# Later loads behind w_k's split, an early Exp table and a later bias split at the start of an attention, MoE and mixer kernel

## The chip, the core and the metric

The kernel runs on one core of a Trainium2 chip. The metric is the device time of one execution in microseconds: 876.57 us is the median of three runs of the kernel before (875.78 to 877.5). One more execution was profiled; it took 876.73 us, of which the trace covers a span of 875.0 us.

## The reference

Three blocks follow each other: causal attention with a cumulative bias, a gated feed-forward block (called MoE in the names) and a token and channel mixer. All numbers are fp32.

```python
def _attn_ref(q, k, v, s):            # 4 batches, 8 heads, 576 tokens, head size 64
    scores = scale * np.matmul(q, k.transpose(0, 1, 3, 2))
    cum = np.cumsum(np.maximum(s, 0.0), axis=-1)
    bias = -(cum[:, :, :, None] - cum[:, :, None, :])
    scores = np.where(causal, -1000000000.0, scores + np.minimum(bias, 0.0))
    attn = softmax(scores)            # written out in the reference
    return np.matmul(attn, v)

def _moe_ref(x, mu_k, mu_r, w_k, w_v, w_r):    # model 512, hidden 1024
    xk = mu_k * x + (1.0 - mu_k) * x_prev      # x_prev: the token before
    xr = mu_r * x + (1.0 - mu_r) * x_prev
    k = np.maximum(xk @ w_k, 0.0)
    return 1.0 / (1.0 + np.exp(-(xr @ w_r))) * (k * k @ w_v)

def _moe2_ref(x, w_tok1, w_tok2, w_ch1, w_ch2):
    u = x + (np.maximum(xt @ w_tok1, 0.0) @ w_tok2).transpose(0, 2, 1)
    return u + np.maximum(u @ w_ch1, 0.0) @ w_ch2
```

## The kernel before, in words

Most products are made of three: both operands are split into a high and a low fp32r word, and high by high, high by low and low by high are summed in PSUM (`products`, line 103). A weight arrives as a raw block and is split in `weight_split` (line 600): ScalarE copies the scaled high halves (line 604 or 607, both through `copy`, line 75) and rewrites the low halves (line 609), VectorE joins them in two passes (lines 610 and 611), ScalarE writes the high words (line 612) and GpSimd the low words (line 616; for w_v VectorE, line 614). Where `ps` is given, the scaled high halves go into one of two PSUM banks (`ps_w`), else back in place into SBUF.

Batch 0's attention is done apart from the rest, head by head, and in two parts. `early` (line 330) takes the first 256 query rows of a head (items j of 0 and 1): scores with the bias as two more rows of the contraction, maximum and mask on VectorE (line 276), Exp on ScalarE (line 287), row sums and normalisation on GpSimd (lines 288 and 290), transposes on TensorE, a copy T on ScalarE and the product with V (line 355). `late` (line 377) takes the other 320 rows, with four bias rows that `split_bias` (line 189) makes and stores in DRAM (`ext_d`). `split_bias` runs in three chunks through a tile `e` of one buffer: GpSimd writes its ones, VectorE its words, and ScalarE's queue issues the store (line 200).

Between them `mix` (line 503) makes HX, the mixed input of w_k's products for two heads at a time. `up` (line 514) multiplies it by w_k; its products are called h. `gate` and `down` (products r and vd) use w_r and w_v. `keep_busy` (line 159) gives TensorE products that nobody reads, here called fillers: 13 at the start, and four behind each early item.

Each engine and each DMA queue takes its instructions in the order in which they stand. That order is made by a scheduler from the data dependences, buffers and the priorities that `at(place)` sets; a lower place comes earlier. Loads are issued on SyncE's queue (SP). The lines of the change: `late_load` (line 364) and `late_values` (line 369) bring q, k, bias and v for a late head, `weight_load` (line 586) a raw weight block. A load can be made to wait by writing a word into its target with an instruction that waits for something, as `behind` (line 156) does. Late head h uses the tile X of slot h % 4; slots 2 and 3 are used before by the early heads 4 to 7. w_k and w_r come in 8 and 4 blocks of 512 KB through five buffers, w_v in 16 blocks through the pool `xt`.

Of the kernel before, what the change touches and what calls it, by code (L numbers as in the profile page):

```python
# [24 lines left out]
def attention_moe_mixer(  # L25
# [118 lines left out]
    xt = {}  # L144
# [13 lines left out]

    def keep_busy(n, x, w):
        idle = ps_t.tile([128, 512], F32, tag="t", name="idle")  # L160
        for _ in range(n):
            nc.tensor.matmul(idle[:, 0:w], x[:, 0:128], x[:, 0:w], start=True, stop=True)
# [26 lines left out]
    def split_bias(cp, cum):  # L189
        n = 3  # L190
        for c in range(n):
            a, z = S * c // n, S * (c + 1) // n
            e = cp.tile([G, 4, 2, z - a], F32R, name="e")
            for r, t in ((1, 1), (3, 1), (0, 0), (2, 0)):
                nc.gpsimd.memset(f32(e[:, r, t, :]), 1.0)
            copy("D", e[:, 0, 1, :], cum[:, a:z])
            nc.vector.tensor_tensor(out=e[:, 2, 1, :], in0=cum[:, a:z], in1=f32(e[:, 0, 1, :]), op=ALU.subtract)
            for x in (0, 2):
                copy("D", e[:, x + 1, 0, :], f32(e[:, x, 1, :]), -1.0)
            nc.scalar.dma_start(out=ext_d[:, :, :, a:z], in_=f32(e))  # L200
# [129 lines left out]
    def early(h, j, V0, cp):  # L330
# [7 lines left out]
        softmax(j, P, mx, 0)  # L338
        if j == 0:
# [24 lines left out]
    def late_load(h):  # L364
        x = late_x[h] = x_tile(h % 4)
        nc.sync.dma_start(out=x[0:D], in_=qk[h])
        nc.sync.dma_start(out=x[D:D + 4], in_=ext_d[h])

    def late_values(p):
        t = v_tile(p % 2)  # L370
        n = S // 128
        nc.sync.dma_start(out=t[:, 0:n], in_=v[0, 0:128 * n, 2 * p * D:(2 * p + 2) * D].rearrange("(t p) d -> p t d", p=128))
# [213 lines left out]
    def weight_load(key, sw, n, pool, tag, q=nc.sync, after=None):  # L586
        r, k, f = sw.shape
        t = pool.tile([128, n, 2], I32, tag=tag, name="raw")[:, 0:k * f].rearrange("p (k f) t -> p k f t", f=f)
        if after is not None:
            behind(after, f32(t[0:1, 0, 0:1, 0]))  # L590
        for r0 in range(0, 128, r):
# [115 lines left out]
    nc.vector.memset(maskc, 0.0)  # L707
    ps_s2, ps_w = open_pool(name="ps_w", bufs=2, space=PSUM, reuse_waits="tile")
    keep_busy(13, maskc, 512)
# [40 lines left out]
    with at(2):  # L750
        split_bias(cp, cum)
    with at(N0 - 5):
        for h in range(4):
            late_load(h)
        for p in range(2):
            late_values(p)
    x = 1.0
    for y, a in enumerate(first):
# [4 lines left out]
        with at(x + 0.6):  # L763
            weight_split((nm, f), W[:, 0, :, f:f + 128], W[:, 1, :, f:f + 128], ps=ps_w)
        x += 1.2
    cp_s.close()
# [12 lines left out]
    for f in range(0, DM, 128):  # L779
        for k in range(0, KF, 2):  # L780
            with at(x):
                weight_load((k, f), rows(w_v, k, k + 2)[:, :, f:f + 128], S // 2, xt_p, "xt")
# [236 lines left out]
```

## Time and profile before

| | |
|---|---|
| median of 3 runs | 876.57 us (875.78 to 877.5) |
| profiled execution | 876.73 us, span 875.0 us |
| TensorE busy | 842.1 us, 96% of the span |
| weight loads of TensorE | 790.2 us, 90% |
| VectorE, ScalarE, GpSimd busy | 480.6, 451.4, 336.9 us |
| share of the chain that ended last | TensorE 37%, ScalarE and VectorE 2% each |

TensorE is the engine that is nearly always busy. A busy share does not say how much work is done: the granted clock has to be read beside it, and fillers count as busy. The page's slices of the span (about 22 us each) show TensorE's gaps in the first three slices and between 140 and 300 us. The DMA line has its highest shares in the first slices too.

### The profile page before, as it was taken

To read this page: it belongs to the slowest core of one execution; us is meant where nothing else is said; L and a number is where in the kernel's file an instruction comes from. 1 tells how busy PE (TensorE), PEld (TensorE's weight loads), DVE (VectorE), ACT (ScalarE), POOL (GpSimd) and SP (SyncE) were. 2 spreads that over 40 slices of the span, in tenths; PEclk is the share of its full clock that TensorE was granted. 3 is DMA by queue.
4 is the path that set the end of the run, shared out by engine and by line. 5 is a ranking of instruction groups with operands and counts; after the bars stand their busy time and mean duration, and the time that the engine had idled before them with its cause. 6 is when DMAs were issued, how large, how long until landed. Compare 5 with 4: busy or idle time off the path is not lost. (4 is left out here: it accounts for less than half of the span.)

```text
span 875.0 us, 17439 instructions
## 1 busy us (share of the span) xinstructions
PE 842.1 (96%) x6125; PEld 790.2 (90%) x6125; DVE 480.6 (55%) x1351; ACT 451.4 (52%) x1256; POOL 336.9 (39%) x600
## 2 busy tenths in 40 slices
PE   7989998988899999999999999999999999999998
PEld 5746767988689999999999989899999999999998
DVE  4877775656769556985469766961331222222221
ACT  3888766856786755868477864840310211211210
POOL 3654766855774644645255854730000000000000
PEclk7989999999999999999999999999999999999999
DMA  7963597887975244431234746562022112112100
GB/s 184 241 169 92 164 248 214 220 229 209 249 196 130 71 106 112 109 91 43 62 104 135 225 150 198 177 197 90 10 85 60 41 34 67 43 37 69 42 25 25
DMA packets 88023, 108.34 MB, mean 124 GB/s; under 512 B 11152, under 2 KB 71568, under 8 KB 87936
## 3 DMA queue, kind: packets, MB, share of 16 engines
q1 hardware_dynamic: 81408, 91.56, 37.6%
q0 software_dynamic: 4576, 15.08, 5.4%
q8 instruction: 48, 0.79, 0.4%
q10 hardware_dynamic: 1952, 0.60, 0.4%
q14 instruction: 39, 0.32, 0.1%
HBM read 77.74 MB, written 28.90 MB: 122 GB/s over the span
## 5 line engine op out<-in xcount | busy, mean ns | idle before, releaser
L858 ACT ACTIVATE HID<-c 128x256 fp32r<-128x256 f32 (+1 forms) x96 | 39.3, 409 | 220.3 <-PE c L108 220.2
L108 PE MATMUL vd<-KK,WV 128*128 128x256 f32 (+1 forms) x768 | 120.2, 300 | 0.9 <-ACT e L536 0.8
L108 PEld LDWEIGHTS vd<-KK,WV 128*128 128x128 f32 x768 | 106.4, 188 | 4.7 <-issue 1.6
L108 PE MATMUL h<-XK,WK 128*128 128x320 f32 (+1 forms) x672 | 105.8, 301 | 3.3 <-ACT k L521 1.9
L290 POOL TENSOR_SCALAR P<-P,sum 128x128 f32<-128x128 f32 (+4 forms) x148 | 91.9, 624 | 42.2 <-DVE sum L289 32.4
L108 PE MATMUL c<-HID,WV 128*128 128x256 f32 (+1 forms) x768 | 104.9, 291 | 0.0
L108 PE MATMUL c<-U,WK 128*128 128x256 f32 (+1 forms) x768 | 103.2, 291 | 1.4 <-DVE HID L859 1.4
L108 PEld LDWEIGHTS c<-HID,WV 128*128 128x128 f32 x768 | 100.6, 188 | 0.0
L108 PEld LDWEIGHTS c<-U,WK 128*128 128x128 f32 x768 | 98.6, 188 | 1.7 <-DVE HID L859 1.6
L108 PEld LDWEIGHTS h<-XK,WK 128*128 128x128 f32 x672 | 93.2, 188 | 5.5 <-ACT k L521 3.3
L287 ACT ACTIVATE P<-P,mx 128x128 f32<-128x128 f32 (+4 forms) x148 | 86.6, 587 | 21.1 <-DVE mx L276 19.3
L859 DVE SCALAR_TENSOR_TENSOR HID<-c,HID 128x256 fp32r<-128x256 f32 (+1 forms) x96 | 43.8, 456 | 81.1 <-ACT HID L858 81.0
L276 DVE CUSTOM_DVE_ANT_0 P<-s,maskc 128x128 f32<-128x128 f32 (+4 forms) x148 | 69.4, 480 | 33.5 <-PE t L430 19.1
L923 DVE TENSOR_TENSOR ut<-c,ut 128x256 f32<-128x256 f32 (+1 forms) x32 | 14.6, 458 | 119.2 <-PE c L108 109.1
L108 PE MATMUL r<-XR,WR 128*128 128x320 f32 (+1 forms) x384 | 61.9, 301 | 0.0
L288 POOL TENSOR_SCALAR sum<-sum 128x1 f32<-128x1 f32 (+1 forms) x148 | 31.8, 215 | 76.2 <-ACT P L287 68.7
L524 POOL TENSOR_TENSOR KK<-k,KK 128x256 fp32r<-128x256 f32 (+1 forms) x64 | 53.7, 844 | 16.1 <-ACT k L523 15.3
L108 PE MATMUL c<-HID,WR 128*128 128x256 f32 (+1 forms) x384 | 54.8, 291 | 0.0
L108 PEld LDWEIGHTS r<-XR,WR 128*128 128x128 f32 x384 | 53.4, 188 | 1.1 <-ACT k L523 0.2
L108 PE MATMUL c<-U,C1A 128*128 128x256 f32 (+1 forms) x384 | 52.8, 296 | 0.1
L108 PEld LDWEIGHTS c<-U,C1A 128*128 128x128 f32 x384 | 51.5, 190 | 0.3 <-ACT U L908 0.3
L108 PEld LDWEIGHTS c<-HID,WR 128*128 128x128 f32 x384 | 51.4, 188 | 0.0
(130 smaller groups left out, 1653.8 us busy)
## 6 DMA issues: line engine op xcount, KB each, us to landing
X<-hl_d SPq DMA_DIRECT2D x72, 288.0 KB
hl_d<-PB SPq DMA_DIRECT2D x48, 288.0 KB
raw<-in_moe_w_ch_dram POOLq DMA_DIRECT2D x48, 256.0 KB, 3.4
PB<-in_qk_dram SPq DMA_DIRECT2D x48, 144.0 KB
yt<-y_d SPq DMA_DIRECT2D x16, 288.0 KB
u_d<-yt SPq DMA_DIRECT2D x16, 288.0 KB
raw<-in_moe_w_k_dram SPq DMA_DIRECT2D x8, 512.0 KB
raw<-in_moe_w_v_dram SPq DMA_DIRECT2D x16, 256.0 KB
```

The lines of the kernel that those rows point to most:

```text
L108: nc.tensor.matmul(ps, a, b, start=first and i == 0, stop=last and i == n - 1)
L276: nc.vector.tensor_tensor_reduce(out=P[0:m, c0:c1], in0=ps[0:m, 0:c1 - c0], in1=mask[0:m], scale=-scale, scalar=3.0e38 if x == 0 else mx[0 ...
L287: nc.scalar.activation(out=P[0:m, 0:w], in_=P[0:m, 0:w], func=AF.Exp, bias=mx[0:m, x:x + 1], scale=-1.0, accum_out=sm[0:m, 0:1])
L288: nc.gpsimd.tensor_scalar(out=sm[0:m, 0:1], in0=sm[0:m, 0:1], scalar1=1e-9, scalar2=1.0, op0=ALU.add, op1=ALU.mult)
L290: nc.gpsimd.tensor_scalar(out=P[0:m, 0:w], in0=P[0:m, 0:w], scalar1=sm[0:m, 1:2], scalar2=1.0, op0=ALU.mult, op1=ALU.mult)
L524: nc.gpsimd.tensor_tensor(out=kk[:, 1, m, 0:n], in0=t[:, 0:n], in1=f32(kk[:, 0, m, 0:n]), op=ALU.subtract)
L858: nc.scalar.activation(out=hi, in_=ps, func=AF.Relu)
L859: nc.vector.scalar_tensor_tensor(out=lo, in0=ps, scalar=0.0, in1=f32(hi), op0=ALU.max, op1=ALU.subtract)
L923: nc.vector.tensor_tensor(out=t, in0=ps, in1=t, op=ALU.add)
```

## The change

Six edits are made together, all at the start of the program.

- `after_block(y, cell)` copies one low word of w_k's block y into a cell on GpSimd. The late loads of heads 0 and 1 and of the values of pairs 0 and 1 get such a word from block 2 in their targets; the w_v loads placed before 20 get one from block 6.
- The late loads' code stands behind that of the weight blocks.
- `split_bias` is called inside `early`, behind the softmax of head 0's first item, and its first chunk waits for a word of that item's tile P.
- An Exp on eight columns of `omu` comes first on ScalarE, so the table is loaded there; `omu` is cleared for it.
- 15 fillers instead of 13 at the start.
- w_r's scaled high halves stay in SBUF instead of a bank.

```diff
+    def after_block(y, cell):
+        nc.gpsimd.tensor_copy(cell, f32(wk[0:1, 1, KD - 1, 128 * y:128 * y + 1]))
...
-    def split_bias(cp, cum):
+    def split_bias(cp, cum, behind):
...
             e = cp.tile([G, 4, 2, z - a], F32R, name="e")
+            if c == 0:
+                nc.gpsimd.tensor_copy(f32(e[0:1, 0, 1, 0:1]), behind)
...
         softmax(j, P, mx, 0)
+        if h == 0 and j == 0:
+            with at(2):
+                split_bias(cp, cum, P[0:1, 0:1])
...
         x = late_x[h] = x_tile(h % 4)
+        if h < 2:
+            after_block(2, x[0:1, 0, 0:1])
...
         n = S // 128
+        if p < 2:
+            after_block(2, t[0:1, 0, 0:1])
+            after_block(2, t[0:1, n, 0:1])
...
+        if gate is not None:
+            after_block(gate, f32(t[0:1, 0, 0:1, 0]))
...
     nc.vector.memset(maskc, 0.0)
+    nc.vector.memset(omu, 0.0)
     ps_s2, ps_w = open_pool(name="ps_w", bufs=2, space=PSUM, reuse_waits="tile")
-    keep_busy(13, maskc, 512)
+    nc.scalar.activation(out=omu, in_=omu, func=AF.Exp)
+    keep_busy(15, maskc, 512)
...
-    with at(2):
-        split_bias(cp, cum)
-    with at(N0 - 5):
-        for h in range(4):
-            late_load(h)
-        for p in range(2):
-            late_values(p)
     x = 1.0
...
-            weight_split((nm, f), W[:, 0, :, f:f + 128], W[:, 1, :, f:f + 128], ps=ps_w)
+            weight_split((nm, f), W[:, 0, :, f:f + 128], W[:, 1, :, f:f + 128], ps=ps_w if nm == "k" else None)
         x += 1.2
+    with at(N0 - 5):
+        for h in range(4):
+            late_load(h)
+        for p in range(2):
+            late_values(p)
...
-                weight_load((k, f), rows(w_v, k, k + 2)[:, :, f:f + 128], S // 2, xt_p, "xt")
+                weight_load((k, f), rows(w_v, k, k + 2)[:, :, f:f + 128], S // 2, xt_p, "xt", gate=6 if x < 20 else None)
```

The scheduler makes a new order of the first third of the program from this. Three places of it follow; line numbers are those of each kernel's own file, the changed one's being 3 to 15 higher.

VectorE at the start, before: the bias row sums (st), the first two chunks of the bias split (e), then the maximum of the first scores (P_161).

```order
L180 SCALAR_TENSOR_TENSOR st<-st 32x320
L77 CAST e<-st 32x192
L77 COPY V_145<-e_129 32x1
L167 TENSOR_SCALAR omu<-mu 128x8
L197 TENSOR_TENSOR e<-st,e 32x192
L79 TENSOR_SCALAR e<-e 32x192 x2
L77 CAST e<-st 32x192
L197 TENSOR_TENSOR e<-st,e 32x192
L79 TENSOR_SCALAR e<-e 32x192 x2
L276 ISA P_161,mx<-s,maskc 128x128
```

The same place of the changed kernel, from omu to the first chunk of the bias split.

```order
L170 TENSOR_SCALAR omu<-mu 128x8
L281 ISA P_165,mx<-s,maskc 128x128
L281 ISA mx 128x1
L281 ISA P_213,mx<-s,maskc 128x256
L281 ISA mx 128x1
L281 ISA P_247,mx<-s,maskc 128x128
L281 ISA mx 128x1
L294 RECIPROCAL sum<-sum 128x1
L281 ISA P_264,mx<-s,maskc 128x256
L281 ISA mx 128x1
L294 RECIPROCAL sum<-sum 128x1
L77 CAST e<-st 32x192
```

The four first maxima have moved ahead of the bias split, whose first chunk now stands behind two row sums' reciprocals.

SyncE's queue from w_k's block 1 on, before; X_544, X_547 and X_550 are the tiles of late heads 0, 1 and 2, ext_d the stored bias rows.

```order
L592 DMA raw<-in_moe_w_k_dram 128x4x256 x4
L366 DMA X_544<-in_qk_dram 64x1152
L592 DMA raw<-in_moe_w_k_dram 128x4x256
L367 DMA X_544<-ext_d 4x1152
L366 DMA X_547<-in_qk_dram 64x1152
L367 DMA X_547<-ext_d 4x1152
L372 DMA VV_556<-in_v_dram 128x4x128
L366 DMA X_550<-in_qk_dram 64x1152
L367 DMA X_550<-ext_d 4x1152
```

In the changed kernel X_651 and X_655 are late heads 0 and 1, X_659 and X_662 late heads 2 and 3, and VS holds the values of a later batch.

```order
L607 DMA raw<-in_moe_w_k_dram 128x4x256 x4
L248 DMA VS<-in_v_dram 128x4x128
L607 DMA raw<-in_moe_w_k_dram 128x4x256
L250 DMA VS<-in_v_dram 64x128 x2
L376 DMA X_659<-in_qk_dram 64x1152
L607 DMA raw<-in_moe_w_k_dram 128x4x256 x2
L376 DMA X_662<-in_qk_dram 64x1152
L376 DMA X_651<-in_qk_dram 64x1152
L377 DMA X_651<-ext_d 4x1152
L376 DMA X_655<-in_qk_dram 64x1152
L607 DMA raw<-in_moe_w_r_dram 128x4x256
```

All eight w_k blocks are now issued ahead of the first late bias row; late heads 2 and 3 stand ahead of heads 0 and 1.

TensorE around the first products h, before; P_945 is a tile of a late head, PT its transposes.

```order
L387 MATMUL s<-X_550 128x384
L387 MATMUL s<-X_550 128x512
L387 MATMUL s<-X_550 64x288
L396 MATMUL t<-ident,P_945 128x128 x3
L416 MATMUL pv<-PT_821,VV_556 64x320 x3
L416 MATMUL pv<-PT_821,VV_556 64x192
L416 MATMUL pv<-PT_821,VV_556 64x64
L387 MATMUL s<-X_550 64x288
L108 MATMUL h<-HX,WK 128x256 x20
```

In the changed kernel the first products h stand among the last early heads; P_503 and P_520 are tiles of early head 6, X_655 is late head 1.

```order
L400 MATMUL s<-X_655 128x384
L165 MATMUL idle<-P_481 128x128 x4
L108 MATMUL h<-HX,WK 128x256 x7
L400 MATMUL s<-X_655 128x512
L108 MATMUL h<-HX,WK 128x256 x5
L400 MATMUL s<-X_655 64x288
L352 MATMUL t<-ident,P_503 128x128
L352 MATMUL t<-ident,P_520 128x128 x2
L363 MATMUL pv<-T,V_149 64x256
L363 MATMUL pv<-T,V_149 64x128
L165 MATMUL idle<-P_503 128x128 x4
L108 MATMUL h<-HX,WK 128x256 x6
```

18 products h have moved from behind the first late PV to places ahead of the last early head's PV.

## Rows read from the trace of the kernel before

**Rows 1.** Stretches: length, busy us (count) of PE, PEld, DVE, ACT, POOL, clock, DMA.

```profile
0.00:8.00 8.00, 6.19 (x19) 2.61 (x19) 3.96 (x13) 0.00 (x0) 3.08 (x19) 1.00 0.44 82
8.00:14.40 6.40, 2.93 (x8) 2.28 (x9) 2.71 (x14) 3.07 (x10) 1.71 (x7) 0.57 1.05 260
14.40:19.70 5.30, 5.30 (x24) 4.90 (x24) 3.05 (x12) 2.05 (x6) 2.66 (x10) 0.55 0.59 184
19.70:48.50 28.80, 28.74 (x189) 22.22 (x188) 23.02 (x76) 25.18 (x65) 18.61 (x35) 1.00 0.94 253
48.50:53.00 4.50, 3.58 (x20) 2.13 (x19) 3.18 (x8) 3.09 (x7) 2.72 (x2) 1.00 1.07 305
53.00:65.07 12.07, 10.16 (x34) 4.41 (x33) 8.94 (x24) 10.87 (x28) 6.50 (x9) 0.72 0.26 83
...
140.00:300.00 160.00, 144.68 (x1035) 135.31 (x1034) 110.43 (x360) 113.42 (x322) 103.71 (x192) 0.99 0.73 197
```

**Rows 2.** Timeline of the start: start, length, instruction, idle time ahead and its releaser.

```profile
5.65 0.15 DVE L167 TENSOR_SCALAR omu<-mu 128x8 f32<-128x8 f32 x1
...
6.86 1.11 PE L336 MATMUL s<-HE 66*128 66x128 f32 x6 [0.53 <-DMA HE<-in_qk_dram]
...
9.42 0.35 DVE L77 CAST e<-st 32x192 fp32r<-32x192 f32 x1 [3.02 <-DMA ext_d<-e]
...
10.57 0.27 DVE L276 CUSTOM_DVE_ANT_0 P<-s,maskc 128x128 f32<-128x128 f32 x1
...
10.91 2.93 PE L336 MATMUL s<-HE 66*128 66x256 f32 x8 [2.93 <-DVE mx L276]
...
11.32 1.28 ACT L287 ACT_TABLE_LOAD   x1 [11.32 <-DVE mx L276]
...
12.62 0.40 ACT L287 ACTIVATE P<-P,mx 128x128 f32<-128x128 f32 x1
...
14.40 0.48 PE L344 MATMUL t<-ident,P 128*128 128x128 f32 x1 [0.56 <-POOL P L290]
```

**Rows 3.** Timeline of ScalarE, the split of w_k's block 0 and T.

```profile
14.38 0.61 ACT L75 ACTIVATE high<-raw 128x512 f32<-128x512 f32 x1
14.93 0.65 ACT L609 ACTIVATE raw<-raw 128x512 uint32<-128x512 uint32 x1
17.05 0.49 ACT L75 ACTIVATE T<-t 128x384 f32<-128x384 f32 x1 [1.46 <-PE t L344]
```

**Rows 4.** Timeline of TensorE, the first fillers, the first PV, later fillers.

```profile
1.25 5.08 PE L162 MATMUL idle<-maskc 128*128 128x512 bf16 x13 [1.25 <-DVE maskc L707]
...
19.70 0.86 PE L355 MATMUL pv<-T,V 128*64 128x256 f32 x4
...
24.32 1.06 PE L162 MATMUL idle<-P 128*128 128x128 f32 x8
```

**Rows 5.** Timeline of DMA issues on the queues of SyncE and ScalarE.

```profile
13.43 0.56 SPq L326 DMA_DIRECT2D X<-e  x1
...
20.00 0.56 ACTq L200 DMA_DIRECT2D ext_d<-e  x1
...
28.99 0.28 SPq L367 DMA_DIRECT2D X<-ext_d  x1
...
37.80 0.53 SPq L592 DMA_DIRECT2D raw<-in_moe_w_k_dram  x1
```

**Rows 6.** Waits of SyncE to 110 us: total, times, longest.

```profile
SPq L367 <- DMA ext_d<-e: 5.3, 1, 5.3
...
SPq L229 <- PE t L396: 2.4, 1, 2.4
...
SPq L326 <- DMA raw<-in_moe_w_k_dram: 0.4, 1, 0.4
```

**Rows 7.** Waits of TensorE from 120 to 300 us.

```profile
PE s L306 <- DMA X<-hl_d: 5.2, 3, 2.0
```

**Rows 8.** Timeline of GpSimd, the low words of w_k's block 2.

```profile
31.23 1.30 POOL L616 TENSOR_TENSOR WK<-raw,WK 128x512 fp32r<-128x512 f32 x1 [0.24 <-ACT WK L75]
```

More of the change, by code (lines that the diff above doesn't have):

```diff
@@ L584, in attention_moe_mixer, with weight_load @@
     raw = {}
-    def weight_load(key, sw, n, pool, tag, q=nc.sync, after=None):
+    def weight_load(key, sw, n, pool, tag, q=nc.sync, after=None, gate=None):
         r, k, f = sw.shape
```

## The prediction

> **What bounds the kernel now.** I read the busy shares first (table above: TensorE 96%), then TensorE in stretches [rows 1]. From 70 us on the largest gap is that between 140 and 300: 15.3 us (160.00 - 144.68). So the end is TensorE's work plus what TensorE loses, and the change leaves its work alone but for two fillers. Its queue differs up to about 300 us and is then the same instruction for instruction; the places that the change is about lie before 70. There the stretches give this loss. Idle: 1.81 (8.00 - 6.19), 3.47, 0, 0.06, 0.92 and 1.91, together 8.17 us. Slow clock, busy time times one minus the granted share: 2.93 x 0.43 = 1.26, 5.30 x 0.45 = 2.39, 10.16 x 0.28 = 2.84, together 6.49 us. That is 14.66 us, the most that anything before 70 us can give back. Between 19.7 and 48.5 nothing is to be had: TensorE is busy 28.74 of 28.80 us at full clock, if in part with fillers (eight records of 1.06 us [rows 4]) that stay in its queue.
>
> Where do the losses come from? The start reads as a chain [rows 2]. The first scores run at 6.86, but VectorE reads them only at 10.57: it stands in front of the second bias chunk until 9.42, because that chunk's one buffer is still being stored (3.02 us, released by the store to ext_d). ScalarE then loads its table at 11.32 (1.28 us) and begins Exp at 12.62; the first transpose runs at 14.40, the first product with V at 19.70 [rows 4], the last part at half clock (0.55 granted is the 1.2 GHz level for nearly all of it). The second loss, 48.5 to 65 us, is waiting for the first w_k products: w_k's blocks 6 and 7 are only issued by 37.80 [rows 5], because SyncE stood 5.3 us before the bias of the first late head [rows 6] and then issued the late loads.
>
> **The change part by part.** I count TensorE's losses after the change, up to the same place.
>
> *Start and fillers.* The first 1.25 us stay [rows 4]. 13 fillers take 5.08 us, 0.39 each; two more cost 0.78 and end at 1.25 + 15 x 0.39 = 7.1, where the first scores began at 6.86. Together 2.03 us.
>
> *Bias split and table.* With the chunks gone from VectorE's front, it reads the first scores at about 7.4 instead of 10.57; without the table load Exp follows it at once instead of 2.05 us later (12.62 - 10.57). The transposes could run near 10. Waits for the three score banks remain: 0.4 (0 to 1), an estimate from the 0.27 us that a read takes. mu_r's load is now issued behind the table load, about 1.5 us later; the instruction on VectorE that needs it, and that stands in front of the first read, ran at 5.65 [rows 2] without a wait, so it can run by 7.2 and is hidden.
>
> *What is late next.* On ScalarE the split of w_k's block 0 still stands before the first copy T of the transposes. SyncE's third bias row waited for that block and went at 13.43 [rows 5, 6]. From there: two passes of 0.55 (14.38 to 14.93 [rows 3], and again), then the store of the first bias chunk, issued by ScalarE (0.56), then T (0.49): the first product with V at 15.6 instead of 19.70, 4.1 us earlier. TensorE's work up to it is 19.70 less its losses there (1.81 + 3.47 + 1.26 + 2.39 = 8.93), 10.77; with 2.03 and 0.4 it is done at 13.2, so it waits 2.4 us (0 if the block lands as much sooner). A wait of 2.93 us stood before the slow clock of before [rows 2]; whether 2.4 us does the same is open: 0 to 2.39, the loss of 14.4 to 19.7; I take 1.2.
>
> *The bias split behind the first tile.* Its waits do not vanish, they move. Each chunk waits until the one before is stored, on VectorE and GpSimd both. With the queues near empty a store took 3.0 us (issue 6.43 to 9.42), behind w_k's loads 9.0 (issued 20.00, waited for until 28.99 [rows 5]). The first store now goes at about 15 and is wanted near 17, the second at about 18, behind four w_k loads, and is wanted near 23: waits of 1 to 7 and of 0 to 4 us on VectorE, with the maxima and mixes of the next heads queued behind, and on GpSimd, with their sums and normalised tiles. In most of this TensorE has fillers and scores of other heads; half of the low middle passes through: 2.0 us (0 to 5.5).
>
> The Trainium skill, "DMA: Bandwidth & Descriptors", section Queues, rings and completion order, says that each DMA engine goes round between the rings of the issuing engines packet by packet; the stores have ScalarE's ring to themselves and would then not stand behind SyncE's weights. The 9.0 us row speaks against it. By the rule the 2.0 us go.
>
> *Loads.* w_k's blocks 6 and 7 now wait only for GpSimd's low words of blocks 1 and 2 and for heads 4 and 5, so they go about 5 us sooner (block 2's were written from 31.23 for 1.30 us [rows 8], block 7 was issued at 37.80), and w_r's blocks follow without the 5.3 us before them. VS's 288 KB ahead of block 5 cost about 1.1 us at the 253 GB/s of that stretch; block 5 has slack. But the order also shows a new wait: the late loads of heads 2 and 3 stand ahead of those of heads 0 and 1, and the last of them waits for TensorE's last early score. Behind it on SyncE are the late heads 0 and 1, all of w_r and w_v. The cells from block 2 are written long before that, so it is this wait and not the gate that holds the first late head. From the last early score to the first late one TensorE has about 4.3 us (three groups of fillers at 1.06, one PV at 0.86 [rows 4] and five transposes); the load needs three issues of 0.5 and 3.0 to 9.0 us. The wait is 0.2 to 6.2; nearer the short end, as w_k is through by then: 1.0.
>
> *First products.* 18 of the products h now stand before the last early heads, so TensorE has work in the stretch that lost 0.92 + 1.91 + 2.84 = 5.67 us. ScalarE has the same work as before up to the last HX, but idled less; TensorE itself becomes the limit. I take 1.5 us of loss left (0 to 5.67).
>
> *Small things.* The one-word copies on GpSimd (one for the bias split, six for the late loads, two for w_v) fall where it is busy 18.61 of 28.80 us [rows 1], so its idle time hides them up to 1 us each; w_r's four high words cost the same pass whether the bank or SBUF takes them, give or take a tenth; the Exp on eight columns lies before 6 us. Nothing on the path.
>
> *Sum.* 2.03 + 0.4 + 2.4 + 1.2 + 2.0 + 1.0 + 1.5 = 10.5 us of loss instead of 14.7: 4.1 us less. From the profiled execution's 876.73 (span 875.0 and 1.73 around it; the median 876.57 is 0.16 lower) this gives 872.6.
>
> **The rivals.**
> 1. The moved waits hide altogether (bias, late load, first products): the losses are 2.03 + 0.4 + 2.4 + 1.2 = 6.0, the gain 8.6, the time 868.1. For it: ScalarE loses its idle time before w_r, and the fillers cover a good deal. Against: VectorE waits for TensorE and TensorE for VectorE at every early head.
> 2. The stores go round with the weights, and only the bias wait is gone: 10.5 - 2.0 = 8.5 of loss, gain 6.1, 870.6. This is the time by the page's rule. Against it the 9.0 us.
> 3. Nothing arrives at the end: between 140 and 300 TensorE already waits 5.2 us for loads of hl_d [rows 7]; if these come when they come, an earlier TensorE waits longer, and about 876 stays. Against: the stage's own loads are started by TensorE (SyncE waited 2.4 us for it before the loads into PB [rows 6]), so they move along.
> 4. Slower: SyncE's wait for the last early score takes the long price. The first late score is then 6.2 us late instead of 1.0, with all late heads, w_r and w_v behind it, and the clock falls again as it did at 53 to 65 us (2.84): the loss is 10.5 - 1.0 + 6.2 + 2.8 = 18.5, 3.9 us more than before, 880.6. It decides from a wait of about 5 us on, where the whole gain is gone.
> That the gate itself does little, since SyncE's order holds the same loads already, changes no time.
>
> **How the numbers follow.** Forecast 0.45, rivals 0.22, 0.10, 0.13 and 0.10. A measurement of this kernel can tell 0.2%, 1.75 us, from no change: faster is below 874.8, slower above 878.3. The forecast with its bounds lies below 874.8 in about nine cases of ten, so faster is 0.41 + 0.22 + 0.10, some 0.74; same 0.15; slower 0.11. The forecast's own range is 870 to 875.5. The range of 866.5 to 878 takes in rivals 1 to 3 and half-way waits, and leaves out rival 4 and the sum of all best ends (864).
>
> **What would show it.** VectorE's first read of scores near 7.4 us and Exp directly behind it; the first T near 15, behind the block's two passes; VectorE and GpSimd waiting for ext_d between 16 and 26; SyncE waiting for TensorE before heads 2 and 3; w_k's blocks 6 and 7 issued before 33; products h before 50 us, and full clock from 20 us on. I am wrong if T isn't held by the block, if TensorE waits over 5 us for the first late head, or if the idle time between 140 and 300 differs from 15.3 by more than 3.

## The result and the profile after

The changed kernel takes 887.53 us (median of six runs, 879.15 to 889.34), against 876.17 us of the kernel before in the same measurement (873.85 to 877.84). The ratio on record is 1.0104, interval 1.0075 to 1.0133 (the two medians alone give 1.0130), so it is 1.0% slower; the forecast was 872.6 us. The profiled execution took 887.15 us, its span is 885.4 us. TensorE is still busy 96% of it.

The stretches of [rows 1] after the change, with the same columns:

```profile
0.00:8.00 8.00, 6.75 (x22) 3.08 (x22) 3.43 (x13) 1.57 (x3) 3.08 (x19) 1.00 0.43 78
8.00:14.40 6.40, 4.87 (x33) 3.81 (x32) 2.91 (x17) 3.23 (x11) 2.99 (x9) 1.00 0.93 245
14.40:19.70 5.30, 5.05 (x35) 4.22 (x36) 4.42 (x16) 3.70 (x11) 3.44 (x9) 1.00 0.93 269
19.70:48.50 28.80, 24.93 (x140) 18.90 (x139) 21.77 (x64) 22.86 (x57) 18.93 (x42) 0.88 0.92 244
48.50:53.00 4.50, 4.50 (x32) 3.43 (x32) 3.59 (x6) 4.24 (x10) 4.05 (x5) 1.00 0.84 219
53.00:65.07 12.07, 7.66 (x38) 5.30 (x38) 11.90 (x20) 6.31 (x16) 6.04 (x7) 0.83 0.09 26
65.07:70.00 4.93, 4.93 (x11) 1.92 (x10) 2.69 (x9) 2.40 (x6) 2.34 (x5) 0.50 0.32 106
140.00:300.00 160.00, 142.68 (x1005) 132.69 (x1006) 109.78 (x349) 108.64 (x309) 103.22 (x191) 0.98 0.74 201
```

The start has what was hoped for: full clock in the first three rows, where before had 0.57 and 0.55. But 19.7 to 48.5, which had been full, now has 3.87 us of idle time and a clock of 0.88; and in 53 to 65 TensorE is busy 7.66 of 12.07 us, while VectorE is busy 11.90. Nearly full and yet late: that is the row to look into.

To compare many kernels, one number per stretch is enough: its length minus busy time times granted clock, the loss. Over the same cuts for both kernels it is (us):

| | 0-20 | 20-45 | 45-75 | 75-140 | 140-300 | 300-600 | 600-end | sum |
|---|---|---|---|---|---|---|---|---|
| before | 9.1 | 0.0 | 5.9 | 0.3 | 16.8 | 5.6 | 3.5 | 41.1 |
| after | 3.0 | 6.8 | 8.8 | 0.0 | 20.2 | 9.2 | 3.5 | 51.5 |

The difference of the sums, 10.4 us, is that of the spans, so for these two traces the losses hold the whole difference. 6.1 us were won ahead of 20; 6.8 and 2.9 were lost up to 75, and 7.0 behind 140.

The measure is coarse. The clock is printed with two decimals, which can move the long column 300-600 by 1.5 us; cut in steps of 2.5 us, the change loses 6.1 instead of 7.0 us more than before behind 140, and 4.6 instead of 3.6 more up to 75. Over all twenty kernels below, the span less the sum of the losses runs from 830 to 836 us. And each trace is one execution: the kernel before alone took 872.49 to 885.35 us in the course of the experiments. A difference of two or three microseconds between two columns is therefore no finding by itself.

The timeline of the start, answering [rows 2, 4] (start, length, instruction, idle time ahead and its releaser):

```profile
1.24 1.28 ACT L725 ACT_TABLE_LOAD   x1 [1.24 <-PEq L1020]
5.48 0.15 DVE L170 TENSOR_SCALAR omu<-mu 128x8 f32<-128x8 f32 x1
7.58 0.29 DVE L281 CUSTOM_DVE_ANT_0 P<-s,maskc 128x128 f32<-128x128 f32 x1 [1.96 <-PE s L341]
7.92 0.40 ACT L292 ACTIVATE P<-P,mx 128x128 f32<-128x128 f32 x1 [5.18 <-DVE mx L281]
9.61 0.27 PE L352 MATMUL t<-ident,P 128*128 128x128 f32 x1
14.65 0.86 PE L363 MATMUL pv<-T,V 128*64 128x256 f32 x4 [1.41 <-ACT T L75]
```

VectorE reads at 7.58 (10.57 before), the transposes begin at 9.61 (14.40), the first product with V runs at 14.65 (19.70), held by T for 1.41 us.

Then GpSimd's queue, TensorE and ScalarE's DMA queue between 17 and 40 us:

```profile
17.59 0.56 ACTq L205 DMA_DIRECT2D ext_d<-e  x1
21.73 0.48 POOL L295 TENSOR_SCALAR P<-P,sum 128x256 f32<-128x256 f32 x1 [0.53 <-DVE sum L294]
25.67 0.95 POOL L200 MEMSET e<- 32x192 f32 x4 [3.47 <-DMA ext_d<-e]
28.28 0.37 POOL L295 TENSOR_SCALAR P<-P,sum 128x128 f32<-128x128 f32 x1
28.48 0.56 ACTq L205 DMA_DIRECT2D ext_d<-e  x1
28.70 0.33 PE L352 MATMUL t<-ident,P 128*128 128x128 f32 x1 [1.72 <-POOL P L295]
38.83 1.74 PE L400 MATMUL s<-X 68*128 68x384 f32 x4 [1.57 <-DMA X<-ext_d]
```

The second bias chunk is stored at 17.59; GpSimd stands 3.47 us for it with the normalisation of the next tile P behind it, and TensorE waits 1.72 us for that P. The last chunk is stored at 28.48 instead of 20.00 [rows 5], and the first late score, which needs it, runs at 38.83 instead of 35.5. But the late store itself holds up little: SyncE waits 0.2 us for it before it issues the bias rows of the late heads, from 32.95 us on.

And the place where VectorE is busy and late, on four engines, 51 to 68 us; L626 and L625 are the two passes that join a raw block, here of w_r, L631 its low words, L295 the normalisation of P:

```profile
51.70 0.68 DVE L626 SCALAR_TENSOR_TENSOR raw<-raw 128x512 int32<-128x512 int32 x1
52.31 0.68 DVE L625 SCALAR_TENSOR_TENSOR raw<-raw 128x512 int32<-128x512 int32 x1
53.02 3.65 DVE L626 SCALAR_TENSOR_TENSOR raw<-raw 128x512 int32<-128x512 int32 x1
57.53 1.79 DVE L626 SCALAR_TENSOR_TENSOR raw<-raw 128x512 int32<-128x512 int32 x1
59.84 0.54 DVE L281 CUSTOM_DVE_ANT_0 P<-s,maskc 128x384 f32<-128x384 f32 x1
51.55 2.05 POOL L295 TENSOR_SCALAR P<-P,sum 64x576 f32<-64x576 f32 x1 [0.28 <-DVE sum L294]
53.58 2.54 POOL L631 TENSOR_TENSOR WR<-raw,WR 128x512 fp32r<-128x512 f32 x2
67.56 0.74 POOL L295 TENSOR_SCALAR P<-P,sum 64x576 f32<-64x576 f32 x1 [0.36 <-DVE sum L294]
56.71 0.70 ACT L75 ACTIVATE WR<-raw 128x512 fp32r<-128x512 f32 x1 [2.67 <-DVE raw L626]
60.45 0.70 PE L400 MATMUL s<-X 68*64 68x288 f32 x2 [4.19 <-DVE mx L281]
67.23 4.36 PE L429 MATMUL pv<-PT,VV 128*64 128x320 f32 x10
```

One and the same pass takes 0.68 or 3.65 us. The long one begins at 53.02, while GpSimd ends its normalisation, and ends at 56.67, 0.55 us after GpSimd's two words of WR (56.12): nearly the time that it takes alone. ScalarE waits 2.67 us for it, the maximum at 59.84 is late, TensorE waits 4.19 us, and its clock then falls (0.50 between 65 and 70 us, the 1.2 GHz level: ten products that take 4.36 us). The reverse is seen too: the same normalisation takes 0.74 us at 67.56, with no pass ahead of it, and 2.05 beside the two passes of 51.70 and 52.31. With a bank, in the kernel before, all 24 passes took 0.66 to 0.69.

### The profile page after: what moved, and what is told of

Read it like the earlier page. It is cut to its first block, busy times and chain, and to the rows that moved or that the text cites. A ratio compares the mean times of both kernels' runs of the same rounds, so it can differ in the third digit from the quotient of the medians.

```text
span 885.4 us, 17479 instructions
## 1 busy us (share of the span) xinstructions
PE 847.0 (96%) x6127; PEld 794.1 (90%) x6127; DVE 488.6 (55%) x1352; ACT 453.5 (51%) x1257; POOL 344.9 (39%) x609
## 5 line engine op out<-in xcount | busy, mean ns | idle before, releaser
L295 POOL TENSOR_SCALAR P<-P,sum 128x128 f32<-128x128 f32 (+4 forms) x148 | 97.1, 659 | 40.4 <-DVE sum L294 32.7
L938 DVE TENSOR_TENSOR ut<-c,ut 128x256 f32<-128x256 f32 (+1 forms) x32 | 14.6, 458 | 119.3 <-PE c L108 101.8
L537 POOL TENSOR_TENSOR KK<-k,KK 128x256 fp32r<-128x256 f32 (+1 forms) x64 | 55.9, 877 | 24.8 <-ACT k L536 23.9
L242 POOL TENSOR_TENSOR PB<-PB 128x288 f32<-128x288 f32 x48 | 40.5, 846 | 31.7 <-ACT PB L75 31.1
L625 DVE SCALAR_TENSOR_TENSOR raw<-raw 128x256 int32<-128x256 int32 (+2 forms) x77 | 41.1, 535 | 21.0 <-ACT raw L624 15.2
```

Source lines behind the costliest of these rows:

```text
L242: nc.gpsimd.tensor_tensor(out=e[:, 0], in0=t, in1=e[:, 1], op=ALU.subtract)
L295: nc.gpsimd.tensor_scalar(out=P[0:m, 0:w], in0=P[0:m, 0:w], scalar1=sm[0:m, 1:2], scalar2=1.0, op0=ALU.mult, op1=ALU.mult)
L537: nc.gpsimd.tensor_tensor(out=kk[:, 1, m, 0:n], in0=t[:, 0:n], in1=f32(kk[:, 0, m, 0:n]), op=ALU.subtract)
L625: nc.vector.scalar_tensor_tensor(out=low, in0=high, scalar=3, in1=low, op0=ALU.logical_shift_left, op1=ALU.bitwise_or)
L938: nc.vector.tensor_tensor(out=t, in0=ps, in1=t, op=ALU.add)
```

## The experiments

The last five columns are losses in us, as above, of the profiled execution. That of run 13 was the slowest of its ten (888.53 us), that of run 15 the fastest of its seven. Run numbers are those of the expectations.

| run | kernel | median us | ratio to before | 0-20 | 20-45 | 45-75 | 140-300 | 300-600 |
|---|---|---|---|---|---|---|---|---|
| 1 | after, w_r in bank | 879.33 | 1.0010 (0.9992-1.0029) | 5.0 | 5.7 | 5.2 | 16.3 | 5.2 |
| 2 | before, w_r in SBUF | 871.97 | 0.9934 (0.9909-0.9958) | 9.1 | 0.0 | 8.6 | 11.2 | 8.5 |
| 3 | before + start | 877.04 | 0.9999 (0.9980-1.0017) | 3.1 | 6.9 | 6.9 | 15.8 | 5.7 |
| 4 | before + loads | 879.75 | 1.0036 (1.0015-1.0057) | 8.4 | 4.0 | 1.9 | 17.6 | 5.9 |
| 5 | run 3, two e | 883.01 | 1.0069 (1.0047-1.0091) | 3.0 | 6.9 | 7.0 | 16.5 | 8.5 |
| 6 | after, two e | 881.38 | 1.0048 (1.0025-1.0070) | 5.3 | 7.3 | 10.5 | 16.1 | 8.7 |
| 7 | before, 14 fillers | 875.39 | 0.9983 (0.9968-0.9998) | 8.6 | 0.0 | 5.6 | 15.9 | 5.2 |
| 8 | after, w_r low on VectorE | 873.65 | 0.9959 (0.9940-0.9979) | 3.7 | 8.3 | 1.4 | 15.5 | 5.6 |
| 9 | run 2, w_r low on VectorE | 880.21 | 1.0043 (1.0020-1.0065) | 8.5 | 0.0 | 8.4 | 18.3 | 5.4 |
| 10 | run 1, w_r low on VectorE | 874.04 | 0.9965 (0.9945-0.9986) | 3.0 | 6.5 | 1.2 | 14.0 | 7.7 |
| 11 | before + table, fillers | 876.57 | 1.0007 (0.9986-1.0029) | 6.5 | 0.0 | 7.4 | 19.7 | 5.6 |
| 12 | after, 14 fillers | 883.26 | 1.0077 (1.0052-1.0101) | 5.4 | 7.8 | 7.1 | 17.6 | 7.8 |
| 13 | after, split at old place | 882.85 | 1.0056 (1.0027-1.0086) | 6.5 | 5.7 | 10.2 | 14.2 | 8.3 |
| 14 | run 13, w_r low on VectorE | 876.53 | 0.9985 (0.9960-1.0011) | 7.3 | 5.9 | 1.8 | 17.4 | 5.8 |
| 15 | after, no gates | 874.17 | 0.9950 (0.9925-0.9974) | 4.1 | 5.3 | 3.1 | 10.9 | 5.9 |
| 16 | before, w_r low on VectorE | 878.09 | 0.9997 (0.9978-1.0015) | 9.2 | 0.0 | 6.0 | 16.7 | 5.1 |
| 17 | run 15, w_r low on VectorE | 877.09 | 1.0000 (0.9981-1.0020) | 3.5 | 5.7 | 5.7 | 13.7 | 8.4 |
| 18 | run 15, w_r in bank | 877.55 | 0.9988 (0.9967-1.0008) | 2.6 | 7.8 | 5.6 | 15.1 | 8.4 |

**Runs 1 and 2: w_r's bank**

```diff
 after:  - ps=ps_w if nm == "k" else None      + ps=ps_w
 before: - ps=ps_w                             + ps=ps_w if nm == "k" else None
```

> The changed kernel with w_r's scaled high halves in a PSUM bank again, all else of the change kept. Theory A (VectorE's passes over w_r, which read and write SBUF alone, are stretched beside GpSimd: 3.65, 1.82 and 1.79 us instead of 0.68, and all that stands behind them on ScalarE and VectorE comes late): the passes take 0.68 us each, TensorE's 4.2 us wait for the maximum at 60 us goes and its slow stretch at 56 to 72 us with it, and the time is 874 to 880 us instead of 887.5. Theory B (the order of the loads, or the moved bias split, costs the time, and the stretched passes lie beside it): 884 to 889 us.

> The kernel before with w_r's scaled high halves kept in SBUF, and nothing else changed. Theory A: the eight passes over w_r average over 1.2 us instead of 0.68, and the time is 880 to 887 us. Theory B: within 2 us of before, 874.5 to 878.5 us. The schedule differs from row 95 of TensorE's queue on, so a difference of 2 to 3 us alone would not decide.

In the changed kernel theory A came out, in the passes and in the time. All 24 passes of run 1 are whole again:

```profile
L625 DVE SCALAR_TENSOR_TENSOR raw<-high,raw x12: 660/682/694, 14.4 to 59.4; 128x512 int32<-128x512 int32 x12
L626 DVE SCALAR_TENSOR_TENSOR raw<-high,raw x12: 666/681/701, 15.3 to 60.7; 128x512 int32<-128x512 int32 x12
```

(minimum, median, maximum in ns). TensorE's wait for the maximum is 0.2 us, and 45 to 75 loses 5.2 us instead of 8.8. But the two spans differ by 9.1 us, and the larger part of that lies behind 140, where the losses are 7.9 us smaller and the theory says nothing. Into the kernel before the SBUF words went alone, and it became 0.7% faster, below both ranges on record, though its passes take up to 2.43 us (1.11 on average) and 45 to 75 loses 2.7 us more. 140 to 300 loses 5.6 us less there. So the stretching is a fact in both, its price hangs on who waits, and the time of the whole on something else as well.

The bank frees the passes, not all of VectorE. An instruction of the mix (L523) that has SBUF operands alone was still held in run 1, beside a word of w_r:

```profile
58.00 1.52 DVE L523 SCALAR_TENSOR_TENSOR t<-xt,omu,t 128x256 f32<-128x256 f32 x1
57.80 1.44 POOL L631 TENSOR_TENSOR WR<-raw,WR 128x512 fp32r<-128x512 f32 x1 [2.67 <-ACT WR L75]
```

It takes 0.48 us in run 10, where no word stands beside it.

**Runs 3, 4, 11 and 13: the start, the loads, and the split's place**

```diff
 run 3 (before):  + split_bias inside early, behind the first tile; + early Exp, omu cleared; + 15 fillers
 run 4 (before):  + late loads' code behind the weights; + after_block gates
 run 11 (before): + early Exp, omu cleared; + 15 fillers
 run 13 (after):  - split_bias inside early      + with at(2): split_bias(cp, cum)
```

> The kernel before with the start of the change alone: Exp table first, 15 fillers, the bias split behind the first tile; loads and w_r as before. Theory A (the start gained its 4 to 5 us and w_r lost them again): 870 to 874 us. Theory B1 (the moved split's waits for ext_d cost more than they give): 880 to 886 us.

> The kernel before with the load edits alone: the late loads' code behind the weights, and the words of w_k's blocks 2 and 6 as gates; start and w_r as before. Theory A: 873 to 878 us, since neither the start nor the bank is touched. Theory B2 (late heads 2 and 3 ahead of 0 and 1 on SyncE, w_r behind them, make the loss): 882 to 888 us.

> The kernel before with the early Exp table and 15 fillers, and the bias split where it was. Theory C2 (in the runs with the start edits the third chunk's store goes at 28.5 to 32.8 us instead of 20.0, so late heads' bias rows land 7 to 19 us later, and this eats the gain): with the split at its old place the store stays ahead of 21 us, the first late score comes by 36 us as before, the table saves up to 1.3 us of the 2.05 between the first read and Exp, and the time is 874 to 876.5 us. Rival C3 (the early stage is bound by ScalarE's and VectorE's work, and whatever is gained at its start is waited for at its end): 876 to 878 us, with the first PV earlier and the last early PV where it was, 50.2 us.

> The changed kernel with the bias split at its old place, all else of the change kept (loads, gates, SBUF words, Exp table, 15 fillers). Theory C2 (the split behind the first tile is what loses 7.3 us between 20 and 45): the loss of 0 to 20 us rises from 3.0 to 6 to 7, that of 20 to 45 falls to 4 or less (the load edits alone lost 4.1 there), and the sum ahead of 45 is no worse than the 10.3 us of the change. The whole: 881 to 886 us if the passes over w_r still fall beside GpSimd. Rival C3 (the early stage ends when it ends, and any start gives 10 to 11 us of loss ahead of 45): the loss of 20 to 45 stays at 6 or more.

Run 3 against run 11 differs in the split's place alone. The stretches, first of run 3, then of run 11 (columns as in [rows 1]), and between them the two waits of run 3:

```profile
0.00:20.00 20.00, 16.87 (x87) 11.06 (x88) 10.75 (x44) 8.47 (x23) 9.48 (x37) 1.00 0.73 179
20.00:45.00 25.00, 21.01 (x122) 16.73 (x121) 18.22 (x55) 18.45 (x49) 14.11 (x29) 0.86 1.10 256
```

```profile
27.56 0.95 POOL L197 MEMSET e<- 32x192 f32 x4 [5.02 <-DMA ext_d<-e]
30.61 0.33 PE L349 MATMUL t<-ident,P 128*128 128x128 f32 x1 [3.29 <-POOL P L292]
```

```profile
0.00:20.00 20.00, 16.29 (x64) 11.16 (x65) 9.95 (x42) 6.99 (x19) 7.99 (x38) 0.83 0.65 170
20.00:45.00 25.00, 25.00 (x165) 19.17 (x164) 21.07 (x69) 21.71 (x58) 17.21 (x32) 1.00 1.01 258
```

The split behind the first tile wins 3.4 us ahead of 20 (6.5 to 3.1) and loses 6.9 from 20 to 45, where the old place loses nothing. In run 3 GpSimd waits 5.0 us for the store, and TensorE 3.3 us for the P behind it. Theory C2 has this right; run 11's time, 876.6 us, is at its upper end and lies in rival C3's range too, but its last early products with V begin 1.2 us earlier than before (48.40 against 49.61), which speaks against C3. In time the two runs can't be told apart (0.9999 and 1.0007): what the split's place costs in its stretch does not show at the end. The load edits lose 4.0 us from 20 to 45 without the start (run 4), but up to 75 no more than the kernel before (14.3 against 15.0), since 45 to 75 loses less. Run 13, with old split and new loads, still loses 5.7, so neither C2 (4 or less) nor C3 (6 or more) was met in it. Runs 3 and 4 came out between the ends that were expected: the parts by themselves cost 0 and 0.4%, the whole 1.0%.

**Runs 5 and 6: two buffers for e**

```diff
- e = cp.tile([G, 4, 2, z - a], F32R, name="e")
+ e = cp.tile([G, 4, 2, z - a], F32R, name="e", bufs=2)
```

> The kernel before with the start of the change alone (as in the third run), but with two buffers for the tile e of the bias split, so that a chunk needn't wait for the store of the one ahead of it. In the third run TensorE lost 7.1 us between 20 and 45 us (4.0 idle, 3.1 of slow clock), behind GpSimd's wait of 5.0 us for that store. Theory C (the store waits, and the slow clock behind them, eat the start's gain): the loss of 20 to 45 falls below 3 us and the time is 870 to 874 us. Theory D (what is gained ahead of 75 us doesn't reach the end, because the order of the work between 140 and 300 us, which the scheduler makes anew, decides): the loss of 20 to 45 falls as well, but the time stays at 875 to 879 us.

> The changed kernel with two buffers for the tile e, nothing else. Theory C: the loss of 20 to 45 us falls from 7.3 to below 3.5 us and the time from 887.5 to 881 to 884 us. Theory D: the first holds, and the time can come out anywhere between 874 and 889, by the losses of 140 to 300 us (16.8 + 3.5 us after the change).

Theory C in this form fell: the loss of 20 to 45 stayed (6.9 and 7.3 us). GpSimd still waits 2.9 us for a store in run 5, and TensorE now waits 3.8 us for the bias rows of a late head; in run 6 it waits 3.7 us for a late head's q and k. The last store did go much sooner, at 17.45 instead of 32.78 us in run 5 (against run 3) and at 17.79 instead of 28.48 in run 6 (against the change), so the late store alone is not what loses the stretch: with the second buffer the waits moved to the late heads' loads. Run 5 also fell outside theory D's range, 6 us above run 3 with the same loss up to 75 (16.9 us in both); the columns behind 140 show 3.5 us of that, and why is not known. Run 6 landed in the 881 to 884 that C gave, but not for C's reason.

**Runs 7 and 12: one filler more, one less**

```diff
 before: - keep_busy(13, maskc, 512)      + keep_busy(14, maskc, 512)
 after:  - keep_busy(15, maskc, 512)      + keep_busy(14, maskc, 512)
```

> The kernel before with 14 fillers at the start instead of 13, nothing else: a change that has no purpose and a known price, 0.39 us. If the time follows from the places that an edit touches, it is 0.4 us above before, 877 to 878 us (ratio 1.000 to 1.001). Theory D: the small shift gives another order between 140 and 300 us, and the time is off by 2 us or more to either side, with the loss of that stretch off by as much.

> The changed kernel with 14 fillers at the start instead of 15, nothing else: again an edit with a known price, 0.39 us. It tells how much of the 887.5 us belongs to the order that happened to come out for 140 to 600 us. If the loss hangs on the edits: 886 to 888 us. Theory D (the order made anew moves the losses of 140 to 600 us by several us; the change drew a bad one, 28.2 us against 22.5 before): 878 to 886 us, with the loss ahead of 140 us unchanged within 1.5 us.

An edit worth 0.39 us moved the kernel before by -0.17% (its interval excludes the +0.05% of the sum). The changed kernel came out at 1.0077 instead of 1.0104; these intervals overlap, so of that alone nothing follows, but the loss of 140 to 600 went from 29.4 to 25.4 us in the traces. Run 12 fell into theory D's range; in run 7 the stretch of 140 to 300 moved by 0.9 us where 2 or more were expected. So theory D holds in weak form at most: some 0.2% can come from a new order alone, by an interval that just excludes no change.

**Runs 8, 9, 10, 14 and 16: w_r's low words on VectorE**

```diff
- nc.gpsimd.tensor_tensor(out=lo, in0=f32(low), in1=f32(hi), op=ALU.subtract)
+ (nc.vector if key[0] == "r" else nc.gpsimd).tensor_tensor(out=lo, in0=f32(low), in1=f32(hi), op=ALU.subtract)
```

> The changed kernel with w_r's four low words written by VectorE instead of GpSimd. Theory A, narrowed after the first two runs (a pass that has all its operands in SBUF is stretched while GpSimd works; that costs the stretch of 45 to 75 us, not the end): of the eight passes over w_r those beside no GpSimd work take 0.68 us, none takes 3.65, and the loss of 45 to 75 us falls from 9.3 to 6 us or less. Rival A0 (the passes are stretched by something else, as the DMA traffic or ScalarE): passes over 1.8 us remain without GpSimd work beside them. The time of the whole is left open between 876 and 889 us by theory D; by theory A alone it is 884.

> The kernel before with w_r's scaled high halves in SBUF and w_r's low words on VectorE, nothing else: no start, no load edits. The run with the SBUF words alone took 872.0 us, with passes of up to 2.43 us beside GpSimd's words of WR and WK. Theory A (VectorE and GpSimd keep each other out when both have all operands in SBUF): passes that fall beside no GpSimd work take 0.68, the loss of 45 to 75 us falls from 8.4 us (second run) to 5 to 6.5, and the time is 868 to 872. Rival A1 (VectorE has no room for the four words and they cost what the passes gave back): 872 to 876.

> The changed kernel with w_r in a bank again and w_r's low words on VectorE. It tells what the eighth run's gain of 14 us came from. Theory A (the passes in SBUF were held by GpSimd): with the bank no pass is stretched anyway, so moving the low words gives nothing beyond the scatter of the order, 877 to 882 us, as the first run with 879.3. Rival A1 (GpSimd itself was the late engine, and four words fewer on it are the gain): 870 to 874 us, as the eighth.

> The kernel of the thirteenth run with w_r's low words on VectorE. If the two losses (the moved split's and that of w_r's passes and words) are separate, they add: it is 8 us or more below the thirteenth and 869 to 873 us, the fastest so far. If GpSimd's four words matter only where the moved split has already made GpSimd late, it is within 3 us of the thirteenth.

> The kernel before with w_r's low words on VectorE and the bank kept, nothing else. With the changed kernel the same edit gave 14 us with the SBUF words and 5 us with the bank; with the kernel before and SBUF words it lost 8 us. Theory A1 (GpSimd's four words hold up the end of the early stage only where GpSimd is late from the moved split): within 3 us of before, 874 to 880 us. Rival (the words are worth it in themselves): 868 to 873 us.

Run 8 is the clearest for the mechanism. VectorE's passes and GpSimd's work in it:

```profile
50.36 1.82 DVE L625 SCALAR_TENSOR_TENSOR raw<-raw 128x512 int32<-128x512 int32 x1
53.44 0.68 DVE L626 SCALAR_TENSOR_TENSOR raw<-raw 128x512 int32<-128x512 int32 x1
54.05 0.68 DVE L625 SCALAR_TENSOR_TENSOR raw<-raw 128x512 int32<-128x512 int32 x1
54.65 0.68 DVE L631 TENSOR_TENSOR WR<-raw,WR 128x512 fp32r<-128x512 f32 x1
55.25 0.68 DVE L626 SCALAR_TENSOR_TENSOR raw<-raw 128x512 int32<-128x512 int32 x1
55.85 0.68 DVE L625 SCALAR_TENSOR_TENSOR raw<-raw 128x512 int32<-128x512 int32 x1
50.32 1.30 POOL L631 TENSOR_TENSOR WK<-raw,WK 128x512 fp32r<-128x512 f32 x1
53.29 3.85 POOL L295 TENSOR_SCALAR P<-P,sum 64x576 f32<-64x576 f32 x1 [0.28 <-DVE sum L294]
```

Seven of the eight passes take 0.67 or 0.68 us; the eighth starts 0.04 us after GpSimd has begun its last word of w_k (1.30 us long), and takes 1.82. Now it is GpSimd that loses: its normalisation needs 3.85 us beside five VectorE instructions of 0.68 in a row (0.74 in the change at 67.56). So in these rows the two engines do not share, they wait for each other's whole instruction, and for several if they come without a gap. The 4.2 us of TensorE are gone, 45 to 75 loses 1.4 us instead of 8.8, and the whole takes 14 us less. That is below every range on record for it (884 by theory A alone): only 7.4 us of the gain lie in that stretch, and the losses behind 140 are 8.3 us smaller.

But the gain is not one of the passes alone: with the bank, where no pass was stretched, the same edit gives 5 us (run 10, at the upper end of A1's range) and again 1.2 us of loss in 45 to 75. With the kernel before it gives nothing (run 16), and with its SBUF words it loses 8 us (run 9, missed by both sides), 7.1 of them between 140 and 300. Run 14 is 6.3 us below run 13, less than the sum of separate losses, more than none.

**Runs 15, 17 and 18: no gates**

```diff
-        if h < 2:
-            after_block(2, x[0:1, 0, 0:1])
-        if p < 2:
-            after_block(2, t[0:1, 0, 0:1])
-            after_block(2, t[0:1, n, 0:1])
-                weight_load(..., gate=6 if x < 20 else None)
+                weight_load(...)
```

> The changed kernel without the words of w_k's blocks 2 and 6 (no gates); the late loads' code still stands behind the weights. The prediction said that the gate itself does little, since SyncE's order holds the same loads: then 884 to 889 us and the first late score at 38 to 40 us as in the change (38.8). Theory B2 (the gates make the late heads late): the first late score comes at 36 us or earlier, and the time is 4 us or more below the change.

> The changed kernel without the gates and with w_r's low words on VectorE: the two single edits gave 874.2 and 873.7 us. If both remove one and the same loss (TensorE's 4.2 us behind the stretched pass and the slow clock after it, 9.3 us in all between 45 and 75 us): they don't add, 871 to 876 us. If they remove different ones: 862 to 868 us.

> The changed kernel without the gates and with w_r in a bank. With SBUF words and no gates two passes of eight were stretched, to 1.12 and 1.31 us, 1.1 us in all. Theory A' (SBUF words cost what their passes are stretched by where TensorE waits for VectorE, and the change's bad place came with the gates): within 2.5 us of the fifteenth run, 872 to 877 us. Rival (the bank is better in itself, as the first run against the change suggested with 8 us): 866 to 870 us.

Without the gates the change takes 874.17 us, 13 us less. Neither reason that was on record is right: the gates do matter, and the first late score comes not earlier but at 47.1 us (38.8 in the change, 35.5 before), when the early products with V are nearly through (last group from 51.1):

```profile
47.06 2.37 PE L395 MATMUL s<-X 68*128 68x384 f32 x6 [1.02 <-DMA X<-ext_d]
51.08 0.86 PE L363 MATMUL pv<-T,V 128*64 128x256 f32 x4
```

The late heads mix with the early ones for some 5 us instead of 15, and no pass over w_r takes over 1.31 us. The edit takes the waits away and also lets the scheduler write another order; which of the two gives the 13 us, this run can't tell. The rows of run 15 for 20-45, 45-75 and 140-300:

```profile
20.00:45.00 25.00, 21.20 (x134) 16.86 (x133) 21.70 (x60) 19.79 (x52) 14.56 (x30) 0.93 1.09 283
45.00:75.00 30.00, 26.90 (x150) 17.52 (x149) 26.74 (x68) 25.26 (x68) 19.58 (x25) 1.00 0.32 93
140.00:300.00 160.00, 149.08 (x1080) 140.62 (x1079) 114.25 (x368) 117.56 (x333) 107.84 (x200) 1.00 0.70 193
```

(This profiled execution took 870.11 us, 4 us less than the median.) Against the change the losses are 5.7 us smaller from 45 to 75 and 12.6 smaller from 140 to 600. Runs 17 and 18 put a second of the three cures on top and come out at 877, so the cures do not add. That each of them ends the same collision of 51 to 60 us fits this; why both come out 3 us above run 15 (the seventeenth 1.1 and the eighteenth 0.5 us above its range), and lose 5.7 and 5.6 us from 45 to 75 where run 15 loses 3.1, is not explained. Run 18 also shows the bank to be no better in itself where the passes hardly meet GpSimd.

## Why the prediction was wrong

*Start and fillers, Bias split and table, What is late next* were right, and better than forecast: 3.0 us of loss ahead of 20 where these steps summed to 6.0, no slow clock, the first product with V at 14.65 where 15.6 was said.

*Bias split behind the first tile* failed in its price. The waits had about the size given (GpSimd 1.0 and 3.5 us, VectorE 0.2 and 2.1, against 1 to 7 and 0 to 4). But "half of the low middle passes through: 2.0 us (0 to 5.5)" left out what an idle TensorE pays afterwards: 6.8 us were lost from 20 to 45, 3.9 of them idle (1.72 before the late P, 1.57 before the late head's bias) and the rest slow clock behind these waits (a granted clock of 0.50 from 31 to 33 us and from 41 to 43, the 1.2 GHz level). That in the full stretch "nothing is to be had" was true; that there was something to lose was not asked. Runs 3 and 11 show the split's place as one cause of the loss in this stretch, run 4 the loads as another (*Loads* allowed 1.0; the wait for the late head's bias was 1.57 us); that either costs as much by the end, no run shows.

*Small things* failed in kind: "w_r's four high words cost the same pass whether the bank or SBUF takes them". What spoke against it was in the trace of before: the smaller passes over w_v, 128x256 with all operands in SBUF, ran between 0.40 and 1.37 us there, those from a bank between 0.66 and 0.69, and the prediction didn't ask what the first ones wait for. The Trainium skill, "SBUF — State Buffer", section "SBUF: two separate sides", says that VectorE instructions with two SBUF inputs and GpSimd instructions that read SBUF exclude each other for a whole instruction. The traces agree: 3.65 us against 0.68 (the change), and 3.85 against 0.74 the other way round (run 8). It was the rule to weigh here.

*First products* failed with it: 1.5 us were given for the stretch that lost 8.8 (to 75 us). The products h did come before 50 us (at 46.43), but behind a VectorE that stood still they cover nothing.

*That the gate itself does little* was wrong: without the gates the kernel is 13 us faster (run 15). With them the first late scores run from 38.8 us, among the early heads and w_r's blocks; without them from 47.1, when the early heads are nearly through. That it is the wait, and not the order that comes with the gates, is not shown.

*The terms were added up*, and the parts do not add. One at a time, on the kernel before, the SBUF words give -0.7% (run 2), the start nothing (run 3) and the loads +0.4% (run 4), together -0.3%; the whole gives +1.0%. What is lost comes from the parts together. Of the three signs of being wrong that were named none came: T stood behind the block's passes, the wait for the first late head was 1.57 us, and TensorE's idle time between 140 and 300 was 17.3 us, 2.0 more than before. What did fail among the other signs is the full clock from 20 us on.

The sum: 18.6 us of loss up to 75 (3.0 + 6.8 + 8.8) where 10.5 were forecast, 8.1 too many; the 7.0 us behind 140, for which no term stood, make it 15.1, and the profiled execution is 14.6 us above the forecast. Rival 4 had the sign but not the place: SyncE did wait for the last early score, but 0.4 us, and TensorE's wait for the late head was 1.57 us, far from the 5 us from which it would decide.

What the 7.0 us behind 140 are is only partly settled. ScalarE and TensorE of the changed kernel around 215 us:

```profile
210.07 0.78 ACT L75 ACTIVATE PB<-PB 128x288 fp32r<-128x288 f32 x2 [7.08 <-DMA PB<-in_qk_dram]
212.03 0.35 PE L501 MATMUL pv<-PF,VV 128*128 128x256 f32 x1 [1.79 <-DVE xt L507]
218.55 0.44 ACT L75 ACTIVATE PB<-PB 128x288 fp32r<-128x288 f32 x1 [3.77 <-DMA PB<-in_qk_dram]
220.07 0.41 PE L501 MATMUL pv<-PT,VV 128*128 128x320 f32 x1 [3.33 <-ACT PT L471]
```

ScalarE stands 7.08 and 3.77 us before raw q and k of a later batch, with the copies that TensorE needs behind it (1.79 and 3.33 us). The kernel before has no such wait over 5.2 us, though all of them together are longer there (31.6 us against 28.7). Over all twenty kernels the loss from 140 to 600 lies between 16.8 and 29.4 us; the change has the highest value, and no single edit goes with it. Each edit that cures the change takes 7.9 to 12.6 us off this part (runs 1, 8 and 15), so half or more of every cure stands on what is not explained here. Whether the new order of these stretches or the later arrival makes it stays open: no run held the order and moved the time alone.

Of all kernels run 2 is the fastest: the one before with w_r's words in SBUF and nothing else, 0.66% below before and 1.7% below the change (its interval overlaps those of runs 8 and 15). Its gain lies between 140 and 300 us; why, no run shows. No combination had a lower median.

## What to carry to other kernels

A gain at the start is worth something only if the next stage can take it: look at what the moved work now stands in front of, and price every new idle time of TensorE with the slow clock behind it. Time the parts of a change by themselves before adding up their terms: here they gave -0.3% and the whole +1.0%. An operand moved from PSUM to SBUF changes who can hold whom, VectorE or GpSimd, even if the instruction takes the same time alone. Where a scheduler writes the order anew, time a neutral edit first: here one filler moved the whole by 0.2%, as much as the verdict sought.

## What the runs showed of the hardware

- An SBUF-only pass of VectorE (128x512 int32, 0.68 us alone) stood through the end of a normalisation and two further instructions of GpSimd behind it (3.65 us), and a GpSimd instruction (0.74 us alone) through five of VectorE (3.85 us): the waiting engine was not let in between them.
- The same pass with one operand in PSUM never took more than 0.70 us in the 24 of run 1, and 0.68 at 51.49 us, beside a GpSimd word of w_r that ran from 51.55 to 52.85.
- After 4.19 us without work TensorE's granted clock fell to 0.50 (the 1.2 GHz level) from 61 us on, and ten products took 4.36 us, against 2.41 in runs 8 and 10; in these, without that wait, 45 to 75 us had a clock of 0.99 and 1.00.
- A bias chunk's store, issued at 17.59 us on ScalarE's queue behind four weight loads of SyncE's, was waited for until 25.67, 8.1 us, and in run 3 9.6 us; the first chunk's store, issued at 13.12 ahead of these loads, was through 3.1 us later. By the rule of rival 2 (the Trainium skill, "DMA: Bandwidth & Descriptors", section Queues, rings and completion order) it would not have stood behind them; these times speak against that, but no run sent the store without the loads.
